# The last unit in pieces over banks of its own, and batch 1's small products two pairs of heads at a time

## The chip, the cores and the metric

One core of one Trainium2 chip. The metric is device microseconds of one execution, as a median of several.

## The reference, cut to what matters

```python
def _attn_ref(q, k, v, g_norm):                      # 8 batches, 8 heads, 576 tokens, 64 wide
    kv = np.einsum('bhsd,bhse->bhde', k, v)
    out = np.einsum('bhsd,bhde->bhse', q, kv)
    rms = np.sqrt(np.mean(out * out, axis=-1, keepdims=True) + 1e-06)
    return out / rms * g_norm

def _moe_ref(x, w_a, w_b, w_out):                    # 4608 tokens, 512 -> 1536 -> 512
    return ((x @ w_a) * (x @ w_b)) @ w_out
```

## The kernel before

A planner inside the kernel takes a list of work nodes (engine, estimated duration, priority, dependencies, buffers taken and freed) and puts each engine's instructions into one fixed order before anything runs. The feed-forward part uses a Strassen-Winograd scheme: each block of 512 tokens costs seven half-size products per level in place of eight, with the sums done by VectorE (DVE) and ScalarE (ACT). Products land in eight PSUM banks, shared out in rings: RX and RY over banks 0 to 3, RO on bank 4, RQ and RS over banks 5 to 7.

The first place that the change touches: batches 0 and 1 arrive in a layout that TensorE (PE) itself transposes, one pair of heads at a time.

```python
def early_qT_mm(self, p, ps):                 # 12 transposes, output on partitions 0-63, then 64-127
    for hl in range(2):
        for c in range(EC):                   # EC = 6
            nc.tensor.transpose(pq[hl * D : (hl + 1) * D, c * EP : (c + 1) * EP],
                                early[self.b]["q"][:, 2 * p + hl, c, :], ident[0:EP, 0:EP])
# early_kv_mm: the same two loops over 12 matmuls k x v, 96 rows, 64 columns
...
# early_batch: one node for each pair
n1 = plan.add("PE", 0.45, pr, lambda p=p, s=sq: at.early_qT_mm(p, s.tile), [got["q"]], [sq])
...
n3 = plan.add("PE", 0.40, pr, lambda p=p, s=sk: at.early_kv_mm(p, s.tile), [got["k"], got["v"]], [sk])
```

The second place: the last unit of the output projection, seven products p1 to p7 of 12 matmuls each (six steps of the sum for each of two row groups, `m = 2`). The results c11, c12, c21 and c22 are the four quarters `o(i, j)` of the unit's output; `ev` copies a bank out, and `comb` adds a bank to what was copied.

```python
p1 = prod(0, X, a11, b11, True, [], [X])
e1 = ev(0, 0, 0, p1, [ob])                            # ACT copies X out
p2 = prod(1, Y, a12, b21, True, [], [Y])
c11 = comb(1, 0, 0, Y, [p2, e1], [Y])                 # DVE adds Y to what was copied
p6 = prod(2, X, sx(s2), t2, False, [e1, n2], (), [s2], 2)     # goes on accumulating in X
e2 = ev(2, 0, 1, p6)
p5 = prod(3, Z, a21, t1, True, [n1], [Z], (), 1)
e5 = ...                                              # ACT copies Z to u5
p7 = prod(4, X, sx(s3), t3, False, [e2, n3], (), [s3], 0)     # X once more, behind the copy e2
e3 = ev(4, 1, 0, p7)
c22 = comb(4, 1, 1, X, [p7, e5], [X, u5], u=u5)
p3 = prod(5, Z, sx(s4), b22, False, [e5, n4], (), [s4], 3)
c12 = comb(5, 0, 1, Z, [p3, e2], [Z])                 # 128x512 in one add
...                                                   # p4 by rows in W[i], c21 by rows, the stores
```

## Time and profile before

| | before |
|---|---|
| median of the first 3 runs | 297.29 us (296.76 to 298.57) |
| span of the profiled run | 294.8 us |
| PE on the chain that ended last | 93% of the span |
| start of the last matmul to the end of the span | 5.27 us |

The lines themselves stand in the prediction. How to read them: a row of the timeline is a run of like instructions, and the printed length of a matmul holds its latency, so its pace is the distance to the next row's start. "Idle before" in brackets says how long the engine waited and what ended the wait. A pause of PE, below, is the time by which the distance between two starts exceeds the pace of the first one's columns; it is longer than the idle time in brackets, which counts only from the end of the printed length.

### The profile page before, as it was taken

Reading aid. Unit: us, or ns where it says so; the run is one execution under the profiler, and the core shown is the slowest. Engines: PE = TensorE matmul, PEld = TensorE weight load, DVE = VectorE, ACT = ScalarE, POOL = GpSimd, SP = SyncE. Lnnn points to the kernel's source line nnn. Section 1 sums busy time; section 2 is a strip of 40 time slices with the busy share of each in tenths; the row PEclk is TensorE's granted clock in tenths of the full one; section 3 lists DMA queues with packets and bytes.
Section 4 is the critical chain, followed back from the end, with each engine's and each line's share of the span. In section 5 each row is a group of like instructions: output and inputs, shape, how many; then the busy total and the mean of one; then the engine's idle time right before and its main releaser. Section 6 shows DMA issues by size and latency. Waiting matters only on the chain.

```text
span 294.8 us, 6757 instructions
## 1 busy us (share of the span) xinstructions
PE 288.1 (98%) x2646; PEld 238.1 (81%) x2648; DVE 240.2 (81%) x441; ACT 191.7 (65%) x395; POOL 77.1 (26%) x96
## 2 busy tenths in 40 slices
PE   8999999999999999999999999999999999999993
PEld 3645558965888988899988998898988888888882
DVE  5454879893987988789979999979989958788852
ACT  3757667876578677877757866786769546665420
POOL 8945830950092470380001910000000000000000
PEclk9999999999999999999999999999999999999999
DMA  8999999699999999499816999330155001200053
GB/s 181 198 199 200 196 158 166 102 168 183 189 128 171 143 170 173 48 136 210 174 31 149 145 166 167 80 145 21 38 85 165 2 0 43 102 2 0 9 172 107
DMA packets 112643, 36.26 MB, mean 123 GB/s; under 512 B 89060, under 2 KB 108516, under 8 KB 112612
## 3 DMA queue, kind: packets, MB, share of 16 engines
q0 software_dynamic: 77552, 18.44, 65.9%
q1 hardware_dynamic: 34448, 16.70, 26.8%
q10 hardware_dynamic: 612, 0.71, 0.8%
q8 instruction: 20, 0.33, 0.5%
q14 instruction: 11, 0.09, 0.1%
HBM read 37.75 MB, written 14.75 MB: 178 GB/s over the span
## 4 chain that ended last, share of the span: by engine, by line
PE 93%; DVE 4%; issue 1%; ACT 1%; DVEq 0%; ACTq 0%
PE bk L839 47%; PE bk L1008 24%; PE bk L387 7%; PE bk L310 3%; PE bk L943 3%; PE bk L624 2%; PE bk L353 2%; PE bk L367 2%; PE bk L341 1%; PE bk L539 1%; PE bk L325 1%; DVE c L858 1%; DVE so L746 1%; DVE o_sb L1046 1%; DVE T L806 1%
## 5 line engine op out<-in xcount | busy, mean ns | idle before, releaser
L858 DVE TENSOR_TENSOR c<-bk,u 128x512 f16<-128x512 f32 x144 | 96.1, 684 | 19.3 <-PE bk L839 11.8
L420 ACT COPY u<-bk 128x512 f32<-128x512 f32 x144 | 81.4, 591 | 36.5 <-PE bk L839 29.9
L839 PE MATMUL bk<-xp,wa_t 128*128 128x256 f16 x288 | 55.0, 273 | 0.1
L839 PE MATMUL bk<-xp,wb_t 128*128 128x256 f16 x288 | 55.0, 273 | 0.0
L839 PEld LDWEIGHTS <-wa_t 128*128 128x128 f16 x384 | 37.1, 98 | 5.7 <-issue 0.3
L1008 PEld LDWEIGHTS <-abt 128*128 128x128 f16 x384 | 37.5, 98 | 4.7 <-issue 0.3
L839 PEld LDWEIGHTS <-wb_t 128*128 128x128 f16 x384 | 37.6, 98 | 4.4
L1008 PE MATMUL bk<-wo_t,abt 128*128 128x256 f16 x288 | 37.2, 273 | 0.1
L839 PE MATMUL bk<-T,sb 128*128 128x256 f16 x192 | 36.7, 273 | 0.0
L839 PE MATMUL bk<-T,sa 128*128 128x256 f16 x192 | 36.7, 272 | 0.0
L420 ACT CAST c<-bk 128x512 f16<-128x512 f32 x48 | 28.0, 587 | 12.1 <-PE bk L839 11.5
L893 DVE TENSOR_TENSOR abt<-c 128x1024 f16<-128x1024 f16 x48 | 32.7, 684 | 0.9
L839 PEld LDWEIGHTS <-sb 128*128 128x128 f16 x288 | 28.2, 98 | 3.3
L839 PEld LDWEIGHTS <-sa 128*128 128x128 f16 x288 | 27.9, 98 | 3.5
L1008 PEld LDWEIGHTS <-as 128*128 128x128 f16 x288 | 28.1, 98 | 3.3
L1040 ACT COPY o_sb<-bk 128x512 f32<-128x512 f32 x31 | 18.2, 586 | 18.5 <-PE bk L1008 18.0
L376 DVE SCALAR_TENSOR_TENSOR xp<-bk,g_col,rs 128x288 f16<-128x288 f32 x40 | 20.2, 512 | 10.9 <-ACT rs L371 10.9
L1008 PE MATMUL bk<-so,as 128*128 128x256 f16 x192 | 25.2, 273 | 0.0
L371 ACT ACTIVATE rs<-bk,eps_t 128x288 f32<-128x288 f32 x40 | 20.0, 506 | 6.2 <-PE bk L367 6.1
L667 POOL DMA_DIRECT2D k_t<-in_k_dram x24 | 21.2, 899 | 0.8 <-issue 0.5
L661 POOL DMA_DIRECT2D scr<-in_q_dram x12 | 19.6, 1638 | 2.5 <-issue 1.5
L1046 DVE TENSOR_TENSOR o_sb<-bk,o_sb 128x512 f32<-128x512 f32 (+1 forms) x25 | 16.4, 663 | 3.0 <-PE bk L1008 2.3
(107 smaller groups left out, 428.8 us busy)
## 6 DMA issues: line engine op xcount, KB each, us to landing
out_dram<-o_sb SPq DMA_DIRECT2D x20, 256.0 KB, 2.7
scr<-in_q_dram POOLq DMA_DIRECT2D x12, 288.0 KB, 8.0
k_t<-in_k_dram POOLq DMA_DIRECT2D x24, 128.0 KB, 8.2
v_t<-in_v_dram POOLq DMA_DIRECT2D x6, 512.0 KB, 11.0
out_dram<-o_sb SPq DMA_DIRECT2D x18, 128.0 KB, 2.4
wa_t<-in_moe_w_a_dram POOLq DMA_DIRECT2D x6, 256.0 KB, 10.6
wb_t<-in_moe_w_b_dram POOLq DMA_DIRECT2D x6, 256.0 KB, 10.8
wo_t<-in_moe_w_out_dram POOLq DMA_DIRECT2D x2, 768.0 KB, 9.7
```

Source lines behind the costliest of these rows:

```text
L371: nc.scalar.activation(rs, self.s_ps[p, h][:, 0:HF], AF.Abs_reciprocal_sqrt, bias=eps_t)
L376: nc.vector.scalar_tensor_tensor(out=xcols(p, self.b * S + h * HF, HF), in0=self.x_ps[p, h][:, 0:HF], scalar=g_col, in1=self.rs[p, h], op0 ...
L387: nc.tensor.matmul(ps[:, 0:n], lhsT=w[:, kc, fc * 128 : (fc + 1) * 128], rhs=xcols(kc, 0, n), start=(kc == 0), stop=(kc == KC - 1),)
L420: ("ACT", act_us(n), lambda: nc.scalar.copy(*args())),
L661: nc.gpsimd.dma_start(out=scr[:, :, hl, :].rearrange("p s d -> s p d"), in_=qv[hl])
L667: nc.gpsimd.dma_start(out=kt[:, c], in_=ks[:, :, c, :])
L839: nc.tensor.matmul(ps.tile[:, i * n : (i + 1) * n], lhsT=lhs(w, sm)[:, kc, :], rhs=rhs()[:, kc, :], start=start and i == 0 and kc == 0, st ...
L858: lambda: nc.vector.tensor_add(cs(fi, h), full(ps), u.tile),
L893: nc.vector.tensor_mul(t, c[:, :, :, 0], c[:, :, :, 1])
L1008: nc.tensor.matmul(ps.tile[:, sub * EH : (sub + 1) * EH], lhsT=lhs(slice(j, j + 1))[:, 0, sub * 128 : (sub + 1) * 128], rhs=rhs[:, j, :], ...
L1040: lambda: nc.scalar.copy(o(fi, h), bank(X, every)), [dep], takes, frees,
L1046: nc.vector.tensor_add(o(fi, h, subs), bank(ps, subs), other)
```

## The change

Its intent: fewer changes between full and small matmuls in batch 1, and a last unit whose evacuation, adds and stores run beside PE's last products instead of after them.

```diff
@@ early_batch: transposes (the kv products get the same treatment, 0.8 us, sk and sk2)
-            n1 = plan.add("PE", 0.45, pr, lambda p=p, s=sq: at.early_qT_mm(p, s.tile), [got["q"]], [sq])
+            if b == 0:
+                n1 = ...                                  # as before
+            elif p % 2 == 0:
+                sq2 = Buf(RQ)
+                n1 = plan.add("PE", 0.9, pr,
+                    lambda p=p, s=sq, s2=sq2: (at.early_qT_mm(p, s.tile), at.early_qT_mm(p + 1, s2.tile)),
+                    [got["q"]], [sq, sq2])
+            else:
+                sq = sq2
@@ last unit
-            e2 = ev(2, 0, 1, p6)
-            p5 = prod(3, Z, a21, t1, True, [n1], [Z], (), 1)
-            p7 = prod(4, X, sx(s3), t3, False, [e2, n3], (), [s3], 0)
-            e3 = ev(4, 1, 0, p7)
-            c22 = comb(4, 1, 1, X, [p7, e5], [X, u5], u=u5)
-            p3 = prod(5, Z, sx(s4), b22, False, [e5, n4], (), [s4], 3)
-            c12 = comb(5, 0, 1, Z, [p3, e2], [Z])
+            e2 = ev(2, 0, 1, p6, (), [X])
+            p7 = prod(P7_AT, V, sx(s3), t3, True, [n3], [V], [s3], 0)        # a bank of its own
+            c2x = ...                                     # DVE: o(1,0) = V + o(0,1)
+            for i in range(m):                            # p5 by rows, Z[i] is a bank each
+                p5 = prod(3 + 0.1 * i, Z[i], a21, t1, True, [n1], [Z[i]], (), 1, subs=rows[i])
+                e5.append(...)
+            c22 = ...                                     # DVE: o(1,1) = o(1,0) + u5, no PSUM
...
+            for i in range(m):                            # p4 and c21 by rows, ahead of p3
+                p4 = prod(5 + 0.1 * i, W[i], a22, t4, True, [n4], [W[i]], subs=rows[i])
+                c21 = comb(5 + 0.1 * i, 1, 0, W[i], [p4, c22], [W[i]], rows[i])
...
+            for i in range(m):                            # p3 and its add by rows, last
+                p3 = prod(6 + 0.1 * i, Z[i], sx(s4), b22, False, [e5[i], n4], (), [s4], 3, subs=rows[i])
+                c12 = comb(6 + 0.1 * i, 0, 1, Z[i], [p3, e2], [Z[i]], rows[i])
+                put(0, rows[i], [c12], queue=("ACT", "SP")[i], es=e2s)
@@
-        (RO, RY, RY, RS, RQ), NJ // 2,
+        (RO, RY, RS, RY, RS, RQ, RY), NJ // 2,
```

More of the change, by code (lines that the diff above doesn't have):

```diff
@@ L423 @@
     T0 = 20.0
+    P7_AT = 2.5
     B5, B6, CX, CY = 5, 8, 3, 4
@@ L508, in early_batch @@
                     )
-            n1 = plan.add(
-                "PE", 0.45, pr, lambda p=p, s=sq: at.early_qT_mm(p, s.tile), [got["q"]], [sq]
-            )
+            if b == 0:
+                n1 = plan.add(
+                    "PE", 0.45, pr, lambda p=p, s=sq: at.early_qT_mm(p, s.tile), [got["q"]], [sq]
+                )
+            elif p % 2 == 0:
+                sq2 = Buf(RQ)
+                n1 = plan.add(
+                    "PE", 0.9, pr,
+                    lambda p=p, s=sq, s2=sq2: (at.early_qT_mm(p, s.tile), at.early_qT_mm(p + 1, s2.tile)),
+                    [got["q"]], [sq, sq2],
+                )
+            else:
+                sq = sq2
             cp, eng, us = (nc.scalar.copy, "ACT", 0.56) if p % 2 and b else (nc.vector.tensor_copy, "DVE", 0.38)
@@ L516, in early_batch @@
             )
-            n3 = plan.add(
-                "PE", 0.40, pr, lambda p=p, s=sk: at.early_kv_mm(p, s.tile),
-                [got["k"], got["v"]], [sk],
-            )
+            if b == 0:
+                n3 = plan.add(
+                    "PE", 0.40, pr, lambda p=p, s=sk: at.early_kv_mm(p, s.tile),
+                    [got["k"], got["v"]], [sk],
+                )
+            elif p % 2 == 0:
+                sk2 = Buf(RS)
+                n3 = plan.add(
+                    "PE", 0.8, pr,
+                    lambda p=p, s=sk, s2=sk2: (at.early_kv_mm(p, s.tile), at.early_kv_mm(p + 1, s2.tile)),
+                    [got["k"], got["v"]], [sk, sk2],
+                )
+            else:
+                sk = sk2
             n4 = plan.add(
@@ L1065, in o_unit @@
         if W:
-            u5 = Buf(RU)
+            u5, V, Z = Buf(RU), W[0], [Z, W[1]]
+            W = W[2:]
+            rows = [slice(i, i + 1) for i in range(m)]
             p1 = prod(0, X, a11, b11, True, [], [X])
@@ L1071, in o_unit @@
             p6 = prod(2, X, sx(s2), t2, False, [e1, n2], (), [s2], 2)
-            e2 = ev(2, 0, 1, p6)
-            p5 = prod(3, Z, a21, t1, True, [n1], [Z], (), 1)
-            e5 = plan.add(
-                "ACT", act_us(m * EH), pr + 3 * du,
-                lambda: nc.scalar.copy(u5.tile[:, every], bank(Z, every)), [p5], [u5],
-            )
-            p7 = prod(4, X, sx(s3), t3, False, [e2, n3], (), [s3], 0)
-            e3 = ev(4, 1, 0, p7)
-            c22 = comb(4, 1, 1, X, [p7, e5], [X, u5], u=u5)
-            p3 = prod(5, Z, sx(s4), b22, False, [e5, n4], (), [s4], 3)
-            c12 = comb(5, 0, 1, Z, [p3, e2], [Z])
+            e2 = ev(2, 0, 1, p6, (), [X])
+            p7 = prod(P7_AT, V, sx(s3), t3, True, [n3], [V], [s3], 0)
+            c2x = plan.add(
+                "DVE", dve_us(m * EH), pr + 4 * du,
+                lambda: nc.vector.tensor_add(o(1, 0), bank(V, every), o(0, 1)), [p7, e2], (), [V],
+            )
+            e5 = []
+            for i in range(m):
+                p5 = prod(3 + 0.1 * i, Z[i], a21, t1, True, [n1], [Z[i]], (), 1, subs=rows[i])
+                e5.append(
+                    plan.add(
+                        "ACT", act_us(EH), pr + 3 * du,
+                        lambda i=i: nc.scalar.copy(u5.tile[:, rows[i]], bank(Z[i], rows[i])),
+                        [p5], [] if i else [u5],
+                    )
+                )
+            c22 = plan.add(
+                "DVE", dve_us(m * EH), pr + 4.2 * du,
+                lambda: nc.vector.tensor_add(o(1, 1), o(1, 0), u5.tile[:, every]), [c2x] + e5, (), [u5],
+            )
             e1s, e2s = slice(0, EH), slice(EH, d_model)
@@ L1086, in o_unit @@
             for i in range(m):
-                put(0, slice(i, i + 1), [c12], queue=("SP", "ACT")[i], es=e2s)
+                p4 = prod(5 + 0.1 * i, W[i], a22, t4, True, [n4], [W[i]], subs=rows[i])
+                c21 = comb(5 + 0.1 * i, 1, 0, W[i], [p4, c22], [W[i]], rows[i])
+                put(1, rows[i], [c21], queue=("ACT", "SP")[i], es=e1s)
             for i in range(m):
-                subs = slice(i, i + 1)
-                p4 = prod(6 + 0.1 * i, W[i], a22, t4, True, [n4], [W[i]], subs=subs)
-                c21 = comb(6 + 0.1 * i, 1, 0, W[i], [p4, e3], [W[i]], subs)
-                put(1, subs, [c21], queue=("ACT", "SP")[i], es=e1s)
+                p3 = prod(6 + 0.1 * i, Z[i], sx(s4), b22, False, [e5[i], n4], (), [s4], 3, subs=rows[i])
+                c12 = comb(6 + 0.1 * i, 0, 1, Z[i], [p3, e2], [Z[i]], rows[i])
+                put(0, rows[i], [c12], queue=("ACT", "SP")[i], es=e2s)
             return
```

## The prediction

> **What bounds the kernel now.** I read the page first: the span, the share of each engine, and the chain that ended last.
>
> ```profile
> span 294.8 us, 6757 instructions
> PE 288.1 (98%) x2646; PEld 238.1 (81%) x2648; DVE 240.2 (81%) x441; ACT 191.7 (65%) x395; POOL 77.1 (26%) x96
> PE 93%; DVE 4%; issue 1%; ACT 1%; DVEq 0%; ACTq 0%
> ```
>
> The chain runs through TensorE (PE) for 93% of the span. So an instruction taken out of PE's stream, or a pause between two of them, is worth its own length, unless another engine then falls behind. What is not PE lies mostly at the end. The change touches two places: batch 1's small matmuls (20 to 35 us) and the last unit (280 us to the end). I read the timeline of PE in the first place, where the distance from one start to the next is the real pace (a matmul's printed duration includes its latency). Columns: start, length, engine, line, operation, output<-input, form, count.
>
> ```profile
> 19.62 1.03 PE L387 MATMUL bk<-xp,wa_t 128*128 128x512 f16 x4
> 20.58 0.56 PE L341 MATMUL bk<-ident,abt 96*64 96x96 bf16 x12
> 21.07 1.04 PE L387 MATMUL bk<-xp,wb_t 128*128 128x512 f16 x4
> 22.04 0.56 PE L341 MATMUL bk<-ident,abt 96*64 96x96 bf16 x12
> 22.53 1.04 PE L387 MATMUL bk<-xp,wa_t 128*128 128x512 f16 x4
> 23.40 0.59 PE L387 MATMUL bk<-xp,wb_t 128*128 128x512 f16 x2
> 23.93 0.66 PE L325 MATMUL bk<-u,abt 96*64 96x64 bf16 x24
> 24.51 0.61 PE L387 MATMUL bk<-xp,wb_t 128*128 128x512 f16 x2
> ```
>
> Twelve transposes (L341, one pair of heads) stand alone between full matmuls; they take 0.49 us to the next start, and the four matmuls ahead of them take 0.96 us, not the 0.865 us of four at 0.216. So each change from full matmuls to the small form costs about 0.10 us more. The kv products (L325) already come 24 at a time, two pairs together. The second half of the batch (30.99, 32.24 and 33.69 us) looks the same. PE pauses nowhere else in this stretch, and the chain is PE throughout.
>
> The same timeline in batch 0, where kv products come one pair at a time, tells what company is worth:
>
> ```profile
> 10.60 0.47 PE L325 MATMUL bk<-as 96*64 96x64 bf16 x12
> 11.00 0.45 PE L310 MATMUL bk<-c 128*128 128x512 bf16 x2
> ```
>
> 12 alone take 0.40 us, 24 together 0.58 us: the second dozen costs 0.18 us.
>
> Then the end, in the timeline of all engines, and the DMA share in three stretches (its last two columns).
>
> ```profile
> 287.64 0.82 PE L1008 MATMUL bk<-so,as 128*128 128x256 f16 x6
> 288.29 1.47 PE L1008 MATMUL bk<-wo_t,as 128*128 128x256 f16 x12
> 288.49 0.59 ACT L1040 COPY o_sb<-bk 128x512 f32<-128x512 f32 x1 [1.16 <-PE bk L1008]
> 289.11 0.69 DVE L1046 TENSOR_TENSOR o_sb<-bk,u 128x512 f32<-128x512 f32 x1 [3.80 <-ACT o_sb L1040]
> 289.72 1.34 DVE L1046 TENSOR_TENSOR o_sb<-bk,o_sb 128x256 f32<-128x256 f32 x3
> 289.83 1.80 SPq L911 DMA_DIRECT2D out_dram<-o_sb  x4
> 290.21 1.29 ACTq L911 DMA_DIRECT2D out_dram<-o_sb  x2
> ...
> 289.50:290.50 1.00, 0.27 (x3) 0.00 (x0) 1.00 (x4) 0.00 (x0) 0.00 (x0) 1.00 0.00 0
> 290.50:293.20 2.70, 0.00 (x0) 0.00 (x0) 0.56 (x1) 0.00 (x0) 0.00 (x0) 1.00 0.88 291
> 293.20:294.80 1.60, 0.00 (x0) 0.00 (x0) 0.00 (x0) 0.00 (x0) 0.00 (x0) 0.56 0.00 0
> ```
>
> PE has no pause in this stretch either. But VectorE (DVE) sits idle for 3.80 us, then has four adds to do in a row from 289.11 to 291.06, because they all come after the copy of p7 (288.49), which itself waits for the second-last product. The last of them, an add of the whole 128x512, ends 1.6 us after the last matmul starts (about 289.5). Six of eight stores then leave within 1.4 us and keep the DMA engines nearly full from 290.5 to 293.2.
>
> **What the Trainium skill says.** "TensorEngine Tiling (Array Packing)", section Key Properties: changing the tiling mode drains TensorE, and different tiles can load weights and multiply in parallel. The trace agrees on both: 0.10 us at each change of form, and 24 products in 0.58 us where twice 12 would need 0.80. "VectorE: DVE Perf Modes", section on the TRN2 errata: an fp32 tensor_tensor takes (N+151)/0.96 ns, 691 ns for 512 and 424 ns for 256; the trace has 0.69 us, and 415 ns for the two 256-wide adds. "DMA: Bandwidth & Descriptors", section Anatomy of one DMA: about 2 us are fixed, mostly the receipt of the write (measured there on the GpSimd path). Here the two stores at 285.3 us, alone on the DMA engines, landed in 1.7 us, and the last six in 2.0 to 2.3 us. So splitting a product into rows costs VectorE 2 x 0.415 instead of 0.69, and a store gains by being alone.
>
> **The change part by part.**
>
> Batch 1. Transposes of two pairs become one group of 24: two groups in place of four. A group of 12 costs 0.49 + 0.10 = 0.59 us now. For the second dozen inside a group I use the kv result: there, 12 more of 64 columns cost 0.18 us, about 15 ns each, which is a bit over half of 64/2.4 = 27 ns. Transposes stream 96 columns, 40 ns, so the second dozen should cost about 12 x 22 = 0.26 us. A group of 24 is then 0.49 + 0.26 + 0.10 = 0.85 us against 1.18: 0.33 us saved, twice, so 0.66 us. The kv products: already adjacent, nothing saved. Copies out of the banks stay the same in number.
>
> Last unit, PE. Seven products of 12 matmuls before and after, 84 x 0.109 = 9.2 us; PE had no pause, so nothing is gained or lost there.
>
> Last unit, the tail. p7 no longer accumulates on X behind e2 but starts a bank of its own, early; its sum and c22 come while PE still has p4 and p3 to do. c21 goes ahead of p3, and p3 ends with a row of six matmuls. After the last matmul's start (289.5) follow 0.33 us to VectorE (as from 288.16, when the last of p7's twelve starts, to the copy at 288.49), one add of 128x256, 0.42 us, and the issue: 290.3 us. Before, the last store was issued at 291.24 (its queue entry ends at 291.63). That is 0.95 us. Two rows of p3, 0.66 us each on PE, leave VectorE time for each 0.42 us add, so it keeps up. The stores of c22 and c21 leave between about 288.2 and 289.2 and are nearly through by 290.8; the last one then lands in about 1.8 us instead of 2.3: 0.5 us more. Tail together 1.45 us.
>
> Sum 0.66 + 1.45 = 2.1 us, all on the path. From 297.29 that makes 295.2. I take off 0.2 for slippage (below): 295.4 us.
>
> **The rivals.**
>
> First: the time won at 20 to 35 us is lost to data that comes by the clock. DMA is at 1.0 or above of its share there, and the queries of batch 1's second half land around 29.9 us, one us ahead of their transposes; joining two pairs means both wait for both banks. For it: weights and later batches load in absolute time. Against it: PE has full matmuls as filler until 43 us, and its only other visible pauses later are 0.27 us at 80.9 and 226.6, where it waits for VectorE, which moves along with PE. If it holds, 0.66 is lost: 296.0.
>
> Second: the static order of the whole kernel comes from a planner that sees different nodes now (0.9 and 0.8 us blocks that need two banks each), and the last unit holds more banks while the last block still needs some. A product that waits for a bank would put a pause of 0.3 to 1 us where there is none. For it: the transposes and the slices of batch 1 share two of the banks. Against: in the last unit Z moves to banks that attention has left, and p4 remains as filler. It would make 296 to 297.
>
> Third: the tail doesn't shorten by more than the add, since the stores are bound by transfer: six of 128 KB at the 291 GB/s of that stretch take 2.7 us. If they are not spread out as I think, the tail wins only 0.95: 295.9.
>
> **Range and chances.** Central 295.4. Low 294.3: the order also loses one of the later pauses, and the second dozen of transposes overlaps better. High 296.7: the batch part or the store part fails, plus some noise; the three runs of before spread 1.8 us. Two per cent is 5.9 us, three times the whole sum: faster 0.02, same 0.97, slower 0.01.
>
> **What would show each step.** Timeline of PE: L341 in two groups of 24 with about 0.75 us to the next start; L325 unchanged at 24 in 0.58; the work at 40 us about 0.6 us earlier. Timeline of the end: one 128x256 add after the last matmul, four of them in all spread at 0.66 us, the idle time before the adds gone; the last store issued 0.8 to 0.9 us after the last matmul's start and landed in 1.7 to 1.9. Wrong if PE shows a new pause over 0.2 us, if L341's groups are split or take 0.97, or if the last landing is still over 2.1 us.

## The result, and the profile after

The changed kernel takes 295.23 us in the median of 6 runs (294.99 to 295.81), the kernel before 297.15 us in 6 (296.76 to 298.79): ratio 0.9925, 95% interval 0.9896 to 0.9954. That is within 2% and 0.17 us under the predicted 295.4.

The first profile of the changed kernel was of its slowest run, 295.81 us, and it is less simple than the medians. Two lines of its page: the span, and the shares of the chain that ended last.

```profile
span 293.7 us, 6760 instructions
...
PE 77%; DVE 9%; DMA 5%; issue 2%; POOL 2%; ACT 2%; SPq 1%; DVEq 0%; ACTq 0%; POOLq 0%
```

The span is only 1.1 us shorter, and PE has fallen from 93 to 77% of the chain, so part of the chain now goes through something else. First the small matmuls, in the timeline of PE:

```profile
20.86 0.81 PE L341 MATMUL bk<-ident,abt 96*64 96x96 bf16 x24
21.60 1.04 PE L387 MATMUL bk<-xp,wb_t 128*128 128x512 f16 x4
...
30.93 0.91 PE L341 MATMUL bk<-ident,abt 96*64 96x96 bf16 x24
31.78 0.39 PE L387 MATMUL bk<-xp,wb_t 128*128 128x512 f16 x1
```

The transposes come in two groups of 24: 0.74 us to the next start in the first, 0.85 in the second. The kv products take 0.58 us (23.87 to 24.45), as before. Then the end, in the timeline of all engines without the weight loads, and the first of the stretches of DMA share that the prediction showed of before:

```profile
288.00 0.69 DVE L1113 TENSOR_TENSOR o_sb<-o_sb,u 128x512 f32<-128x512 f32 x1
288.65 1.47 PE L1029 MATMUL bk<-wo_t,as 128*128 128x256 f16 x12
288.72 2.26 SPq L932 DMA_DIRECT2D out_dram<-o_sb  x4
288.79 1.13 DVE L1067 TENSOR_TENSOR o_sb<-bk,o_sb 128x256 f32<-128x256 f32 x3
290.16 0.42 DVE L1067 TENSOR_TENSOR o_sb<-bk,o_sb 128x256 f32<-128x256 f32 x1 [0.23 <-PE bk L1029]
```

```profile
289.50:290.50 1.00, 0.62 (x6) 0.30 (x4) 0.77 (x3) 0.00 (x0) 0.00 (x0) 1.00 0.84 280
```

The last matmul starts at 289.85 us (288.65 plus eleven steps of 0.109), one add of 0.42 us follows 0.31 us later, and the DMA engines have been moving the other stores since before then: the first of the last six was issued at 288.72 us, 1.13 us ahead of the last matmul's start (before, at 289.83, 0.34 us behind it). From the last matmul's start to the end of the span it is 3.83 us, against 5.27.

So the end is 1.44 us shorter and the transposes save about half a us, yet this one span is only 1.1 us shorter. Of the missing 0.9 us, 0.28 went into a later first matmul with the second weight matrix (16.59 us, 16.31 before) and 0.09 into a wait at 60.7 us for a chunk of `wo_t`. The rest is in the chain of this execution around 190 us:

```profile
182.11 3.74 DMA xs<-xt
...
193.29 0.57 ACT c L420
...
193.91 1.57 PE bk L860 x12
```

A store of a late batch's activations was issued 0.45 us later than in the kernel before and took 3.74 us (3.08 before); the transposing DMA behind it and ACT's work came late, and PE paused 0.46 us, and 0.10 us once more at 194.9. A new pause over 0.2 us was on the prediction's list of signs that it is wrong. Is this one the price of the time won early, or bad luck of one execution? That was the first question for the runs.

### The profile page after: what moved, and what is told of

It reads as the page before. It is cut to its first block, busy times and chain, and to the rows that moved or that the text cites. A ratio compares the mean times of both kernels' runs of the same rounds, so it can differ in the third digit from the quotient of the medians.

```text
span 293.7 us, 6760 instructions
## 1 busy us (share of the span) xinstructions
PE 286.7 (98%) x2646; PEld 237.5 (81%) x2648; DVE 241.4 (82%) x443; ACT 191.3 (65%) x395; POOL 77.7 (26%) x96
## 4 chain that ended last, share of the span: by engine, by line
PE 77%; DVE 9%; DMA 5%; issue 2%; POOL 2%; ACT 2%; SPq 1%; DVEq 0%; ACTq 0%; POOLq 0%
PE bk L860 40%; PE bk L1029 21%; PE bk L387 7%; PE bk L964 3%; DVE c L879 3%; DMA wb_t<-in_moe_w_b_dram 3%; PE bk L645 2%; PE bk L353 1%; PE bk L367 1%; SPq L615 1%; DMA xs<-xt 1%; POOL as L242 1%; DVE xt L593 1%; ACT xp L621 1%; DMA xp<-xs 1%
## 5 line engine op out<-in xcount | busy, mean ns | idle before, releaser
L914 DVE TENSOR_TENSOR abt<-c 128x1024 f16<-128x1024 f16 x48 | 32.8, 687 | 0.9
L1061 ACT COPY o_sb<-bk 128x512 f32<-128x512 f32 x30 | 17.6, 586 | 17.3 <-PE bk L1029 16.8
L371 ACT ACTIVATE rs<-bk,eps_t 128x288 f32<-128x288 f32 x40 | 20.1, 507 | 6.4 <-PE bk L367 6.2
```

Of the source, the lines that this page charges most:

```text
L371: nc.scalar.activation(rs, self.s_ps[p, h][:, 0:HF], AF.Abs_reciprocal_sqrt, bias=eps_t)
L914: nc.vector.tensor_mul(t, c[:, :, :, 0], c[:, :, :, 1])
L1061: lambda: nc.scalar.copy(o(fi, h), bank(X, every)), [dep], takes, frees,
```

## The experiments

All in rounds of five. last_whole, p7_on_x and the two late_wb runs were made on another chip, where the kernel before has a median of 297.01 us, not 297.1; their ratios are to that. The two right columns are from each run's profile: from the first matmul with the second weight matrix `wb_t` (about 16.3 us, see below) to the last matmul's start, and from there to the end of the span.

| kernel | median us | ratio (95% interval) | `wb_t` to last matmul | last matmul to end |
|---|---|---|---|---|
| before | 297.1 | 1 | 273.18 | 5.27 |
| changed, first profile | 295.23 | 0.9925 (0.9896 to 0.9954) | 273.25 | 3.83 |
| after_again | 295.14 | 0.9935 (0.9921 to 0.9948) | 272.60 | 3.84 |
| pairs_only | 296.48 | 0.9984 (0.9972 to 0.9997) | 272.74 | 5.26 |
| tail_only | 295.51 | 0.9953 (0.9940 to 0.9966) | 273.19 | 3.83 |
| alternate | 295.14 | 0.9936 (0.9924 to 0.9949) | 272.53 | 3.83 |
| last_whole | 295.67 | 0.9962 (0.9948 to 0.9977) | 272.60 | 4.48 |
| p7_on_x | 296.12 | 0.9977 (0.9965 to 0.9989) | 272.60 | 5.38 |

My theory was that two savings, 0.55 us in the transposes (read from the first profile; 0.66 was predicted) and 1.45 us in the tail, add up and stay. The rivals were that the early one is given back to DMA, and that within the tail only one of its two ingredients matters.

**after_again: the changed kernel once more.** No edit.

> The changed kernel once more, to see whether the 0.46 us pause at 193 us (a wait for the column scaling of a transposed batch) belongs to the kernel or to that one execution. Theory (the savings of 0.55 us in the transposes and 1.45 us in the tail add up and stay): ratio 0.9935, 295.2 us, and PE at the last matmul about 0.2 to 0.6 us earlier than before. Rival (the time won early is given back at 193 us every time): the pause of about 0.4 us is there again and PE's last matmul starts no earlier than 289.5 us.

The span is 292.8 us, and the chain has PE back at 89%:

```profile
PE 89%; DVE 3%; DMA 3%; POOL 2%; issue 1%; ACT 0%; ACTq 0%; POOLq 0%
```

There is no pause at 193 us beyond the 0.07 us that the kernel before has too, and the last matmul starts at 289.0 us, 0.5 us earlier than before. The rival falls as stated: the pause doesn't come every time. Nor is it in the profiles of the next five rows of the table. It isn't unique, though: in the profile of late_wb_alternate (below) a transposing DMA took 3.26 us, not 2.73, and PE paused 0.22 us at 194.1, and 0.11 us at 195.1, for the same instructions of ACT.

**tail_only and pairs_only: one part of the change each.** The edit of the first puts the old `early_batch` back into the changed kernel; the second puts the new one into the kernel before.

```diff
# tail_only = changed kernel with
-            elif p % 2 == 0: ... (two pairs in a node)
+            n1 = plan.add("PE", 0.45, ...)      # one pair in a node; n3 likewise
# pairs_only = kernel before with the opposite of this
```

> The kernel before with the new last unit alone. Theory: the tail is worth 1.45 us, so about 295.7 us, ratio 0.995; from the last matmul's start to the end about 3.85 us, against 5.27 before. Rival (stores bound by transfer): 0.95 us, ratio 0.997.

> The kernel before with batch 1's pairs joined and the old last unit. Theory: 0.55 us less (four groups of transposes at 0.59 become two at 0.84 and 0.95), so about 296.6 us, ratio 0.998. Rival (lost to data that comes by the clock): the work at 40 us is earlier but a pause later in the trace takes it back, ratio 1.000.

The tail alone gives 0.9953 (1.4 us) and the pairs alone 0.9984 (0.5 us). Their sum, 0.0047 + 0.0016 = 0.0063, meets the 0.0065 of both together in after_again; each interval is about 0.0013 to either side, 0.4 us, so for the pairs the clock alone says only 0.1 to 0.8 us. The profiles place them cleanly: the tail moves only the last column of the table, the pairs only the one before it. That goes from 273.18 to 272.74, 0.44 us and not 0.57: 0.12 us were lost again in one wait at 60.5 us for the first chunk of `wo_t`, which landed at 60.44. So the rival was right there for a fifth of the gain; in after_again the chunk landed at 60.32 and cost nothing.

**last_whole: the rows of the last product undone, and with them those of p5, which shares its banks.** p7 keeps its own bank.

```diff
-            for i in range(m):
-                p5 = prod(3 + 0.1 * i, Z[i], ..., subs=rows[i])   # and e5, p3, c12 by rows
+            p5 = prod(3, Z, a21, t1, True, [n1], [Z], (), 1)
+            e5 = [one 512-wide copy]
...
+            p3 = prod(6, Z, sx(s4), b22, False, e5 + [n4], (), [s4], 3)
+            c12 = comb(6, 0, 1, Z, [p3, e2], [Z])
```

> The changed kernel with p5 and p3 again whole in one bank each, one 512-wide copy and one 512-wide last add; p7 keeps its own bank and c21 stays ahead of p3. So only the rows of the last product are undone. Theory (the rows are worth the shorter add, 0.69 against 0.42 us, and a little at the store because both rows leave at once): from the last matmul's start to the end 4.1 to 4.3 us instead of 3.84, about 295.5 us, ratio 0.9948. Rival (the rows carry the tail's gain, p7's bank little): 4.8 us or more, ratio 0.997.

```profile
287.78 1.47 PE L1029 MATMUL bk<-wo_t,as 128*128 128x256 f16 x12
288.44 1.90 SPq L932 DMA_DIRECT2D out_dram<-o_sb  x4
288.52 1.46 DVE L1067 TENSOR_TENSOR o_sb<-bk,o_sb 128x256 f32<-128x256 f32 x3
```

The end takes 4.48 us, more than I expected and less than the rival's 4.8. The last add again starts 0.31 us after the last matmul, but takes 0.69 us, so the last store is issued 0.23 us later (1.03 us after the last matmul's start, not 0.80). The larger part is in the stores: both rows' stores leave together behind those of c21, and from the last issue to the end it takes 3.45 us against 3.03. So the rows, of p5 and p3 together, are worth 0.23 + 0.42 = 0.65 us, and p7's bank with c21 ahead of p3 the other 0.79; those two were not taken apart. Nor does the run show that the 0.42 comes from the last two stores alone. With p5 whole, c22 is added later, and the first of the last six stores leaves only 0.54 us ahead of the last matmul's start, not 1.13. From that first store's issue to the end of the span it is 4.93 us before, 4.96 in the changed kernel, 5.02 here and 5.20 in p7_on_x, and from the first packet of the six stores to the last it is 2.52, 2.56, 2.56 and 2.75 us. So the end of the span may follow the first of these stores as much as the last add. The two moved together in every run; one that delays c22's store alone would tell.

**p7_on_x: p7's own bank undone.** The rows of the last product stay.

```diff
-            e2 = ev(2, 0, 1, p6, (), [X])
-            p7 = prod(P7_AT, V, sx(s3), t3, True, [n3], [V], [s3], 0)
-            c2x = plan.add("DVE", ..., lambda: nc.vector.tensor_add(o(1, 0), bank(V, every), o(0, 1)), ...)
+            e2 = ev(2, 0, 1, p6)
+            p7 = prod(P7_AT, X, sx(s3), t3, False, [e2, n3], (), [s3], 0)
+            c2x = ev(4, 1, 0, p7, (), [X])
```

> The changed kernel with p7 again accumulating on X behind the copy of p6, and its sum again a copy by ScalarE; the rows of the last product stay. So only p7's own bank is undone. Theory (the bank frees VectorE from doing four adds after PE's end): the copy comes 1.3 us before PE's end, c22 and both c21 run after the last matmul's start and push the last add back by 0.65 us, the stores bunch a little: 4.5 to 4.8 us from the last matmul's start to the end, about 295.9 us, ratio 0.9962. Rival (the rows carry the gain): 3.85 to 4.1 us, ratio 0.994.

```profile
287.68 1.47 PE L1029 MATMUL bk<-wo_t,as 128*128 128x256 f16 x12
287.88 0.59 ACT L1061 COPY o_sb<-bk 128x512 f32<-128x512 f32 x1 [1.54 <-PE bk L1029]
288.60 0.42 DVE L1067 TENSOR_TENSOR o_sb<-bk,o_sb 128x256 f32<-128x256 f32 x1 [3.91 <-PE bk L1029]
288.94 0.68 DVE L1110 TENSOR_TENSOR o_sb<-o_sb,u 128x512 f32<-128x512 f32 x1
289.54 1.08 DVE L1067 TENSOR_TENSOR o_sb<-bk,o_sb 128x256 f32<-128x256 f32 x3
```

All of the tail's gain is gone: 5.38 us, a little worse than the 5.27 of before. DVE sits idle for 3.91 us, then does five operations in a row, almost the picture of the old kernel. The direction was expected, the size (4.5 to 4.8) wasn't. The planner put the first row's add ahead of c22, which waited for it (288.60), so the last add starts 1.33 us after the last matmul. The order alone costs little: with c22 first, the same five operations at the paces of these lines would put the last add about 0.13 us earlier, an estimate; it is the queue of five that costs. And the stores then queue at their issuers, so that the last one goes out 0.47 us after that add ends. Rows with no bank of their own for p7 gain nothing; the bank (with c21 ahead of p3) without rows gains 0.79 us; both gain 1.44. The rows pay only once the queue of adds in front of the last one is gone.

**alternate: the two column tiles in turn.**

```diff
-            for hl in range(2):
-                for c in range(EC):
+            for c in range(EC):
+                for hl in range(2):
```

> The changed kernel, with the loops of the small matmuls in batches 0 and 1 turned round, so that neighbours alternate between the two column tiles instead of six in one tile and then six in the other. If the order of issue decides how much of two tiles overlaps, a group of 24 transposes shrinks from 0.74 to about 0.6 us and a group of 12 from 0.49 to about 0.35, 0.3 to 0.8 us in all: ratio 0.991. If PE's queue already lets the second tile start early, as the starts within a group of before suggest (the second tile's first start comes 0.11 us after the first's), at most 0.1 us per group is won: ratio 0.993.

```profile
20.94 0.70 PE L341 MATMUL bk<-ident,abt 96*64 96x96 bf16 x24
21.57 1.04 PE L387 MATMUL bk<-xp,wb_t 128*128 128x512 f16 x4
...
16.67 0.61 PE L387 MATMUL bk<-xp,wb_t 128*128 128x512 f16 x2 [0.55 <-DMA wb_t<-in_moe_w_b_dram]
```

The first group of 24 shrinks from 0.74 to 0.63 us, a group of 12 from 0.49 to 0.38, and kv groups by 0.07 to 0.09, so the order of issue does count, by 0.1 us a group. But the time didn't change. In batch 0 the gain turns into a longer wait for the first chunk of `wb_t`, which lands by the clock: the first matmul with it starts between 16.28 and 16.76 us, at most 0.05 us after the landing, in all the kernels of the table. In batch 1, PE now pauses 0.29 us before the second kv group, 0.09 of it the usual change of form: the v it needs was issued at 22.2 us and landed 11.1 us later, at 33.3, and the group starts at 33.38. That is the clock again; in after_again the same load landed at 32.8 us and its group started at 33.20, so the changed kernel has little room left there. A shorter pause, 0.09 us inside the second group of transposes, ends with ACT (L371, which reads a bank), and I read that as the second pair's bank coming free. In the changed kernel that second group takes 0.10 us longer than the first, with no pause that the timeline prints. It is the same wait: in all six profiles of the table with joined pairs, the 13th transpose of that group starts 0.05 us after the end of that ACT instruction.

**late_wb and late_wb_alternate: more work ahead of that landing.** The planner is told that the first chunk of `wb_t` lands later, so that it orders other work first; the second run alternates the tiles too.

```diff
-        "b": dict(zip(range(FC), (15.0, 15.0, ...
+        "b": dict(zip(range(FC), (16.4, 16.4, ...
```

> The changed kernel, whose planner is told that the first chunk of the second weight matrix lands 1.4 us later (it does land at 16.3 to 16.7 us in all six traces, and PE waits 0.2 to 0.6 us for it there). The order then puts two small fillers and the third and fourth product of the first matrix ahead. Theory (PE is bound from that landing on, so work moved ahead of it counts fully): 0.1 to 0.4 us less, 294.9 us, ratio 0.992. Rival (the moved work is itself not ready then, or another order of the whole plan costs as much): ratio 0.9935 or above.

> The same with the small matmuls alternating between the two column tiles. In the run with that alone every group became 0.06 to 0.11 us shorter, but two new waits of 0.3 and 0.2 us took it back (for a bank before the second kv group, for wb in batch 0). Theory: with a later wb in the plan a part of it stays, 294.7 us, ratio 0.9915. Rival: the wait before the second kv group stays, ratio as without alternating.

(The expectation calls the wait before the second kv group one for a bank; the trace shows v's landing, as told above.) Both gave a wrong result (relative error 0.185, the same in both), so neither is a version to use; the cause stays open. Their times say nothing for the idea either: 295.39 us (0.9945) and 295.16 us (0.9936). The first matmul with `wb_t` came at 17.10 and 17.28 us, 0.33 and 0.70 us after the chunk's landing, and a new 0.40 us pause for ACT stood at 77 us in both. In the second, the pause before the second kv group was there again, 0.43 us for v's landing, as the rival had it. So no version tried here is faster than the changed kernel.

## Why the prediction was right

- **What bounds the kernel.** PE's stream, with its own length the price of everything removed: right. The transposes of after_again save 0.57 us on PE, and from the first matmul with `wb_t` the last one came 0.58 us earlier (273.18 to 272.60).
- **Transposes, 0.66 us.** The mechanism was right, the term a little large. The first group of 24 saved 0.34 us as worked out (0.74 us measured, 0.75 estimated from the kv products). The second took 0.85, so 0.23: together 0.57 us. The estimate left out that the second pair has to find its bank free (0.05 us behind ACT, and the overlap of the two pairs lost with it). This is the second rival in a small form, 0.1 us instead of 0.3 to 1.
- **kv products, nothing.** Right: 0.58 us per 24 before and after.
- **PE in the last unit, nothing.** Right: no pause over 0.06 us appears there in any of the profiles.
- **The tail, 1.45 us.** 1.44 us measured, and its two terms as well: the last issue 0.94 us earlier relative to the last matmul (1.74 to 0.80, predicted 0.95), and from that issue to the end 0.49 us less (3.52 to 3.03, predicted 0.5). The third rival's number, 0.95 us, did not come true, but its mechanism isn't refuted: from the first packet of the six stores to the last it is still 2.56 us (2.52 before), and what changed is that the first of them leaves 1.47 us earlier against the last matmul. The reasons given for the second term were only in part right. The other stores were not "nearly through by 290.8": on the prediction's clock, with the last matmul at 289.5, the changed kernel issued them from 288.4 to 289.65 and their packets ended at 291.4, 0.36 us ahead of the last store's. That the size came out as predicted is partly luck.
- **The first rival, time lost to data that comes by the clock.** It didn't take the gain of batch 1 in the repeated run. It is real where I hadn't looked: `wb_t`'s landing at about 16.5 us varies by half a us between executions and moves everything after it, and it ate what alternating tiles won in batch 0, as the landing of v did in batch 1. It took 0.12 of the pairs' 0.57 us in pairs_only, at `wo_t`'s landing. And a slow DMA cost 0.46 us at 193 us in the first profile and 0.22 us in that of late_wb_alternate; the other profiles of the changed kernel and its variants have no such pause.
- **The slippage of 0.2 us.** None was needed: 0.58 + 1.44 = 2.02 us of the traces against 0.9935 x 297.1 = 295.2, so 1.9 us by the clock. That 295.4 came within 0.2 us is partly luck: the sum was 0.09 too large and 0.2 were taken off it, while the base of three runs, 297.29, lay 0.2 above the 297.1 of nine.
- One detail was wrong without cost: the four 256-wide adds aren't spread 0.66 us apart. Three run together, and only the last waits for PE. Nor do all four adds of the kernel before depend on the copy of p7: the last one needs p3, and was late only because it stood behind the others in DVE's order.

## What to carry to other kernels

When one engine fills the span, look for the end, where other engines work alone: let the last product end in a bank whose add depends on nothing else that is late, make the last add and store small, and let the stores ahead of them leave early (which of these two counted for more is open here). Free the adds in front of it first, because splitting the last piece while a queue still stands before it gained nothing here. And time won ahead of a transfer that lands by the clock is only won if nothing later waits for that transfer.

## What the Trainium skill lacked or had wrong

- "TensorEngine Tiling (Array Packing)", section Key Properties, says that a change of tiling mode drains TensorE but gives no figure. Here, ahead of a group of 96x64 matmuls, the step from the last full 128x128 matmul is 0.310 us where it is 0.216 between two full ones, 0.094 us longer, at every such change in batch 1 of the kernel before.
- "TensorE: Matmul & The Clock Gate", section The mechanism (Part 3), says that matmuls start and end in program order, strictly. With two column tiles the starts in the trace are out of order. In batch 0 the program has 12 transposes (L341) and behind them 12 kv products (L325); the profile of after_again shows the first products starting ahead of the last transposes:

```profile
6.70 0.47 PE L341 MATMUL bk<-ident,so 96*64 96x96 bf16 x10
6.98 0.22 PE L325 MATMUL bk<-as 96*64 96x64 bf16 x2
7.01 0.21 PE L341 MATMUL bk<-ident,so 96*64 96x96 bf16 x1
```

- The same page, section Measured speedup vs the span model, has measured speedups for tiles of 32 rows or columns, none for two column tiles of 64 with many matmuls each. Here the second dozen kv products costs 0.18 us against 0.40 for the first, and alternating the tiles instead of six and six saves another 0.1 us per group.
- "DMA: Bandwidth & Descriptors", section Anatomy of one DMA, fits 2.0 us plus bytes over 436 GB/s for the GpSimd path, so 2.3 us for 128 KB by that estimate; it has no such fit for stores issued by SyncE or ScalarE. Those land here in 1.7 us when alone, in 1.8 us as the last of the changed kernel (0.64 us behind its neighbour), and in 2.0 to 2.3 us when six leave within 1.4 us.
